# Values from weights three steps old, and in front of the scores, in a fused top-k attention and SMeLU MLP kernel

## The chip, the cores and the metric

The kernel runs on one core of one Trainium2 chip. The metric is device time in microseconds (us), lower is better: the median of the timed runs is 1606.17 us (three runs, 1605.85 to 1606.31).

A core has engines with queues of their own: TensorE (PE, with its weight loads shown apart as PEld), VectorE (DVE), ScalarE (ACT), GpSimd (POOL) and SyncE (SP), which here issues all DMAs. Each engine works through its instructions in program order and waits at an instruction until its semaphores are there.

## The reference

Eight batches of eight heads, 576 tokens of 64 numbers each; everything is float32. In each row of the scores only the 32 largest count. The attention's output, heads side by side, is the input of an MLP of 4608 x 512 x 2048 x 512 with a smoothed ReLU between.

```python
scores = scale * np.matmul(q, k.transpose(0, 1, 3, 2))           # (8, 8, 576, 576)
kth = np.partition(scores, -32, axis=-1)[..., -32:-31]
scores = np.where(scores >= kth, scores, -1000000000.0)
attn = np.exp(scores - np.max(scores, axis=-1, keepdims=True))
attn = attn / (np.sum(attn, axis=-1, keepdims=True) + 1e-09)
x = np.matmul(attn, v).transpose(0, 2, 1, 3).reshape(4608, 512)
h = x @ w_in                                                     # 512 -> 2048
g = np.where(h >= 1, h, np.where(h <= -1, 0.0, (h + 1) ** 2 / 4))
return g @ w_out                                                 # 2048 -> 512
```

## The kernel before

The attention is cut into 144 *steps*. A step takes 128 rows of queries of two heads (the 576 rows of a head are four tiles of 128 and a tail of 64; the tails of four heads share a step). For each step there are, in this order:

- *scores* (`scores`, L272): eight matmuls `sp`, two PSUM tiles, copied and scaled to `s` by ACT (L287);
- the *top 32* on DVE (`weights` and `first_top`, L310 and L345): the first part of step m+1 (`more` and `less`, L300, the first maxima, and ACT's `nmax` and `Exp` into `e`, L321 and L323) is woven into the last part of step m. It ends with L386, which zeroes what lies below the 32nd value and sums the rest;
- *division* by the sum on POOL (`divide`, L339), in the first place of the next step;
- *transposition* of the weights: in most steps by DMA (`move_w`, L412). ACT splits `e` into 16-bit halves (`halves`, L416, two copies), SP writes them to DRAM as `rows` (L418), and a transposing DMA brings them back as `wT` (L419). In the early steps and the last two it is done by TensorE (`transpose_w`, L395, with a diagonal matrix `diag` that ACT makes, L336);
- *values* (`values`, L425): 20 matmuls, or 40 short ones for tails, into a PSUM tile `po`, which ACT copies to `xT` (L446, L448).

When all heads of 128 rows are through, the rows are a *chunk* (36 in all), and `mlp` (L457) puts its MLP work into a queue `pending`: 8 hidden groups (`ph`, eight matmuls; then `r` and `g` by ACT and POOL, L470 to L484) and 16 output products (`py`, one matmul each, L489; then ACT copies `y`, L492, and SP stores it, L494). The last eight output products of the chunk before are woven in behind the first four hidden groups, two behind each; so when only those are left, a new chunk's first hidden group comes next on PE.

The order of PE, DVE, ACT and POOL is written out by the loop at L661; the order of SP is made by the framework's scheduler. A step has seven *places* (`slot` 0 to 6, so the third place is slot 2). Each place takes a part of the top-k work, then what is due there, and ends with `advance`, which takes MLP work from `pending` by a planned share. In the late steps (after all weights are converted, `early` false) the places of the loop before are:

- place 2: transposes of the next queries (`pq`) and, every second step, of the next batch's keys (`pk`, `pkt`); ACT copies them to `qT` and `kT`;
- place 3: `move_w` of step m-1;
- place 4: in odd steps the inspection of a piece of the weights' high words (`inspect_piece`, two `Sign` instructions with a sum, L168); in even steps the load of the next piece (`raw`, L126);
- place 5: the scores of step m+2, then the values of step m-2.

PSUM tiles: `sp`, `pq`, `pk`, `pw` share two buffers (tag "a"); `ph` and `po` share three; `py` has one. `s` and `e` have three buffers, `wT` has two in the late steps.

Of the kernel before, what the change touches and what calls it, by code (L numbers as in the profile page):

```python
# [10 lines left out]
F32 = mybir.dt.float32  # L11
# [3 lines left out]
AF = mybir.ActivationFunctionType  # L15
# [9 lines left out]
def kernel(  # L25
# [10 lines left out]
    nc = tc.nc  # L36
# [3 lines left out]
    P = 128  # L40
# [79 lines left out]
    def load(pool, i, bufs=3):  # L120
        if i < n_pieces and i not in loaded:
            if room and i < 28:
                loaded[i] = room[i % 8]
            else:
                loaded[i] = pool.tile([P, 2 * WC], U32, name="raw", bufs=bufs)
            nc.sync.dma_start(out=loaded[i], in_=pieces_of_weights[i][1].bitcast(U32))  # L126

    def words_of(pool, i, bufs=3):
        load(pool, i, bufs)
        words = loaded.pop(i).rearrange("p (n t) -> p n t", t=2)  # L130
        return words[:, :, 0], words[:, :, 1]
# [30 lines left out]

    def inspect_piece(pool, i):

        _, hi = words_of(pool, i, 2)
        for x in range(2):
            sign = pool.tile([P, WC], F32, name="sign", bufs=1)
            nc.scalar.activation(sign, hi.bitcast(F32), AF.Sign, bias=tiny[:, x:x + 1],  # L168
                                 accum_out=signs[:, x, i:i + 1])


    def run(ctx, paired):
# [157 lines left out]
        def divide(st):  # L330
            rz = att.tile([P, 2], F32, name="rz")
            nc.vector.reciprocal(rz, st["z"])
            if st["by_tensor"]:
                st["rz"] = diag = (late or words).tile([P, 2, P], F32, name="diag", bufs=1)
                for i in range(2):
                    nc.scalar.activation(diag[:, i, :], ident, AF.Copy, scale=rz[:, i:i + 1])  # L336
            else:
                for i in range(2):
                    nc.gpsimd.tensor_scalar(st["e"][:, i, :], st["e"][:, i, :], rz[:, i:i + 1], 1.0, ALU.mult, ALU.mult)  # L339
            if paired:  # L340
                m, seconds, kth = st["m"], st["seconds"], st["kth"]
                nc.gpsimd.tensor_tensor(out=excess[:, 2 * m:2 * m + 2], in0=seconds[:, 8:9 + SPLIT:SPLIT], in1=kth[:, LAST:7:-SPLIT],
                                        op=ALU.subtract)
# [50 lines left out]

        def transpose_w(st):  # L395
            w = st["e"]
            st["wT"] = wT = (late or words).tile([P, BLOCKS, P], F32, name="wT", bufs=2 if late else 1)
            pt = ps.tile([P, 2, NT, P], F32, name="pw", tag="a", bufs=2)
            for i in range(2):
                for c in range(NT):  # L400
                    nc.tensor.matmul(pt[:, i, c, :], w[:, i, main(i)][:, c * P:(c + 1) * P], st["rz"][:, i, :],  # L401
                                     start=True, stop=True)
            for i in range(2):
                nc.scalar.copy(wT[:, i * (NT + 1):i * (NT + 1) + NT], pt[:, i])
            pt = ps.tile([P, P], F32, name="pwt", tag="a", bufs=2)
            for i in range(2):
                nc.tensor.matmul(pt[i * TL:(i + 1) * TL, :], w[:, i, tail(i)], st["rz"][:, i, :], start=True, stop=True)
            nc.scalar.copy(wT[:, NT], pt)
# [1 line left out]


        def move_w(st):  # L412
            st["wT"] = wT = late.tile([P, BLOCKS, P], F32, name="wT", bufs=2)
            halves = late.tile([P, 2, 2 * S], U16, name="halves")
            for i in range(2):
                nc.scalar.copy(halves[:, :, i * S:(i + 1) * S], st["e"][:, i, :].bitcast(U16).rearrange("p (k t) -> p t k", t=2))  # L416
            rows = dram.tile([P, 2, 2 * S], U16, name="rows")
            nc.sync.dma_start(out=rows, in_=halves)  # L418
            nc.sync.dma_start_transpose(wT.bitcast(U16), rows.rearrange("p t k -> (p t) k"))  # L419
# [37 lines left out]
        def mlp(xT, rows, pool, last):  # L457
            gs, group = {}, 1 if last else GROUP
            py = []

            def hidden(x):
                ph = ps.tile([P, group, P], F32, name="ph", tag="ph", bufs=3)
                for i in range(group):
                    f = x * group + i
                    for kk in range(NK):
                        nc.tensor.matmul(ph[:, i], w_in[:, kk, f * P:(f + 1) * P], xT[:, kk],  # L466
                                         start=(kk == 0), stop=(kk == NK - 1))

                r = pool.tile([P, GROUP, P], F32, name="r", bufs=2)[:, 0:group]
                nc.scalar.activation(r, ph, AF.Relu, bias=half, scale=0.5)  # L470
                gs[x] = g = pool.tile([P, GROUP, P], F32, name="g", bufs=2 * LAG)[:, 0:group]
                if last:
                    nc.vector.tensor_scalar(g, ph, -1.0, 0.0, ALU.add, ALU.max)
                    nc.scalar.activation(r, r, AF.Square)
                    nc.vector.scalar_tensor_tensor(out=g, in0=r, scalar=1.0, in1=g, op0=ALU.min, op1=ALU.add)
                    return
                nc.scalar.activation(g, ph, AF.Relu, bias=minus, scale=1.0)  # L477
                if converted < n_pieces and x % 2:
                    nc.scalar.activation(r, r, AF.Square)
                    nc.gpsimd.tensor_scalar(r, r, 1.0, 0.0, ALU.min, ALU.max)  # L480
                else:
                    nc.gpsimd.tensor_scalar(r, r, 1.0, 0.0, ALU.min, ALU.max)  # L482
                    nc.gpsimd.tensor_tensor(out=r, in0=r, in1=r, op=ALU.mult)  # L483
                nc.gpsimd.tensor_tensor(out=g, in0=r, in1=g, op=ALU.add)  # L484

            def final(f):
                if f == 0:
                    py.append(ps.tile([P, DM], F32, name="py", tag="py", bufs=1))
                nc.tensor.matmul(py[0], gs[f // group][:, f % group], w_out[:, f, :], start=(f == 0), stop=(f == NF - 1))  # L489
                if f == NF - 1:  # L490
                    y = (late or words).tile([P, DM], F32, name="y", bufs=2)
                    nc.scalar.copy(y, py[0])  # L492
                    for p0, p1, dst in rows:
                        nc.sync.dma_start(out=dst, in_=y[p0:p1])  # L494

            behind = []
            while pending and pending[-1][3]:
                behind.insert(0, pending.pop())  # L500
            for x in range(NF // group + LAG):
                if x < NF // group:
                    pending.append((NK * group, needed(x * group + group - 1, False), partial(hidden, x), False))
                if x < LAG:
                    for _ in range(min(GROUP, len(behind))):
                        pending.append(behind.pop(0)[0:3] + (False,))
                else:
                    for f in range((x - LAG) * group, (x - LAG + 1) * group):
                        pending.append((DM // P, needed(f, True), partial(final, f), x >= NF // group))
# [151 lines left out]
        for m in range(n + 2):  # L661
# [6 lines left out]

            share, left = (total - spent) / (n + 2 - m), sum(x[0] for x in pending)
            for r in sorted(ready):  # L670
                if r + 3 > m and r >= valued:
                    share = min(share, left / (r + 3 - m))
                    left += NK * NF + NF * DM // P
            top_k, parts = None, [0] * SLOTS
            if m < n:
# [7 lines left out]
            for slot in range(SLOTS):  # L683
# [3 lines left out]
                if m < n and converted < n_pieces:  # L687
                    if slot in now_converting:
                        convert(now)
                elif slot == 3 and late is not None:  # L690
                    if m % 2:
                        inspect()
                    elif paired:
                        load(late, inspected, 2)
                if slot == 1 and 1 <= m <= n and state[m - 1]["by_tensor"]:
                    pe_time = max(pe_time, done[m - 1] + 2.0) + 1.0
                    transpose_w(state[m - 1])
                    ready_at[m - 1] = pe_time + 1.8
                if slot == 2 and 1 <= m <= n and not state[m - 1]["by_tensor"]:
                    move_w(state[m - 1])  # L700
                    ready_at[m - 1] = done[m - 1] + 14.0
                if slot == 2 and m == n and paired:
                    judge(ps, att)
                if slot == 2 and (early or m == first_late or m >= n - 1):
                    values_until(m)
                if m == 0 and slot in (1, 2):
                    next(first)
                if slot == 4:
                    begin_at(m + 2)
                    if not early:  # L710
                        values_until(m - 1)
                if slot == (6 if early else 1):
                    queries(m + 3)
                    if m < n and prep is None and next_keys < B and steps[m][0] == next_keys - 1 and steps[m][1] >= 1:
# [61 lines left out]
```

## Time and profile before

| | us |
|---|---|
| median of the timed runs | 1606.17 |
| the profiled execution | 1610.32 |
| its span, first to last instruction | 1608.5 |
| PE busy | 1514.0 |
| DVE busy | 1422.1 |
| ACT busy | 1140.4 |
| POOL busy | 943.3 |

The mean granted TensorE clock is 0.977 of full speed: 0.78 in the first 100 us, 0.90 in the second, 1.00 from there to 1400 us and 0.98 after.

How to read it: the page gives busy time, share of the span and instructions per engine, then the span in 40 slices (a digit is a busy share in tenths). A row of a group has the line, engine and operation, output<-input by the program's names, shapes and count, then busy time, mean ns of one, and the idle time of the engine in front of them with what ended it. A matmul in float32 leaves two records, so 8 instructions of `ph` are 16 records. Matmuls overlap, and a mean of one is longer than the distance of two. A row of a timeline has start, length, and in brackets the idle time before it.

### The profile page before, as it was taken

What the parts mean: (1) busy time and instruction counts of PE and PEld (TensorE: products, weight loads), DVE (VectorE), ACT (ScalarE), POOL (GpSimd) and SP (SyncE); (2) the same over time, 40 slices, a digit from 0 to 9 for tenths busy, and PEclk for the clock granted to TensorE, in tenths of its full rate; (3) what the DMA queues carried; (4) which work ended last, traced back from release to release, by engine and by line L of the source; (5) the groups of instructions that cost most, each with busy time, mean ns of one, the idle gap of its engine ahead of it and who ended that gap; (6) DMA issues with size and microseconds to landing.
All of it is one profiled execution on the core that took longest, in us unless ns stands there. A gap on an engine that the chain in (4) does not pass through costs nothing.

```text
span 1608.5 us, 32395 instructions
## 1 busy us (share of the span) xinstructions
PE 1514.0 (94%) x10925; PEld 1080.7 (67%) x10925; DVE 1422.1 (88%) x4443; ACT 1140.4 (71%) x2308; POOL 943.3 (59%) x1376
## 2 busy tenths in 40 slices
PE   5587999999999999999999999999999999999988
PEld 4465676777667776777667767766666667666665
DVE  7999889999998998999999998999898998889932
ACT  5677567777777767777768877776677776677632
POOL 5766466666555665655556666555555665556640
PEclk7798999999999999999999999999999999999999
DMA  9433246565465556665565545655565555544410
GB/s 252 132 96 110 72 130 174 157 158 153 133 174 161 154 143 173 161 150 145 145 172 159 160 133 157 172 143 140 135 174 146 142 142 130 145 131 126 123 51 16
DMA packets 439056, 227.92 MB, mean 142 GB/s; under 512 B 393056, under 2 KB 401248, under 8 KB 438880
## 3 DMA queue, kind: packets, MB, share of 16 engines
q1 hardware_dynamic: 438880, 225.75, 51.8%
q8 instruction: 88, 1.44, 0.4%
q14 instruction: 88, 0.72, 0.1%
HBM read 62.91 MB, written 86.11 MB: 93 GB/s over the span
## 4 chain that ended last, share of the span: by engine, by line
PE 71%; ACT 13%; POOL 4%; DVE 4%; DMA 4%; issue 3%; SPq 1%; POOLq 0%; ACTq 0%; DVEq 0%
PE ph L466 27%; PE py L489 24%; PE sp L285 8%; PE po L433 7%; ACT halves L416 3%; ACT e L323 3%; DMA wT<-rows 2%; ACT s L287 2%; ACT sign L168 2%; PE pw L401 1%; POOL e L339 1%; POOL r L483 1%; PE po L441 1%; ACT r L470 1%; POOL g L484 1%
## 5 line engine op out<-in xcount | busy, mean ns | idle before, releaser
L466 PEld LDWEIGHTS ph<-xT,w_in 128*128 128x128 f32 x4608 | 554.4, 192 | 118.3 <-issue 79.8
L466 PE MATMUL ph<-xT,w_in 128*128 128x128 f32 x4608 | 576.1, 278 | 14.8 <-ACT xT L446 12.9
L489 PE MATMUL py<-w_out,g 128*128 128x512 f32 x1152 | 558.6, 601 | 7.3 <-ACT y L492 7.1
L482 POOL TENSOR_SCALAR r<-r 128x256 f32<-128x256 f32 x276 | 150.7, 546 | 526.5 <-ACT r L470 526.1
L307 DVE MATCH_REPLACE8 more<-tops,more 128x288 f32<-128x288 f32 x864 | 375.2, 437 | 0.0
L416 ACT COPY halves<-e 128x1152 uint16<-128x1152 uint16 x260 | 288.0, 1153 | 112.7 <-POOL e L339 111.5
L470 ACT ACTIVATE r<-ph,half 128x256 f32<-128x256 f32 (+1 forms) x296 | 139.0, 470 | 241.1 <-PE ph L466 227.9
L489 PEld LDWEIGHTS py<-w_out,g 128*128 128x128 f32 x1152 | 193.5, 191 | 137.0 <-issue 131.2
L386 DVE SCALAR_TENSOR_TENSOR e<-s,kth,e 128x577 f32<-128x577 f32 x288 | 249.2, 900 | 0.1
L484 POOL TENSOR_TENSOR g<-r,g 128x256 f32<-128x256 f32 x280 | 219.6, 784 | 22.0
L323 ACT ACTIVATE e<-s,nmax 128x576 f32<-128x576 f32 x288 | 217.4, 770 | 4.7
L339 POOL TENSOR_SCALAR e<-e,rz 128x576 f32<-128x576 f32 x260 | 218.6, 851 | 0.0
L483 POOL TENSOR_TENSOR r<-r 128x256 f32<-128x256 f32 x276 | 201.5, 730 | 23.0
L300 DVE TENSOR_TENSOR more<-s 128x576 f32<-128x576 f32 x144 | 114.9, 798 | 109.0 <-ACT s L287 108.6
L287 ACT ACTIVATE s<-sp 128x576 f32<-128x576 f32 x288 | 169.2, 638 | 4.5 <-PE sp L285 4.2
L285 PE MATMUL sp<-kT,qT 64*128 64x288 f32 x1024 | 162.0, 433 | 9.9 <-ACT kT L244 9.0
L285 PEld LDWEIGHTS sp<-kT,qT 64*128 64x128 f32 x1024 | 89.6, 188 | 98.9 <-issue 29.1
L433 PE MATMUL po<-wT,v_in 128*64 128x128 f32 x2048 | 145.9, 282 | 10.3 <-DMA wT<-rows 7.9
L433 PEld LDWEIGHTS po<-wT,v_in 128*64 128x64 f32 x2048 | 113.4, 139 | 60.5 <-issue 37.5
L477 ACT ACTIVATE g<-ph,minus 128x256 f32<-128x256 f32 x280 | 131.8, 471 | 0.0
L348 DVE MAX8 tops<-more 128x8 f32<-128x288 f32 x288 | 125.4, 442 | 0.0
L300 DVE TENSOR_TENSOR less<-s 128x576 f32<-128x576 f32 x144 | 117.4, 815 | 0.0
(92 smaller groups left out, 1528.2 us busy)
## 6 DMA issues: line engine op xcount, KB each, us to landing
rows<-halves SPq DMA_DIRECT2D x130, 576.0 KB, 2.8
raw<-in_moe_w_out_dram SPq DMA_DIRECT2D x52, 256.0 KB, 2.8
raw<-in_moe_w_in_dram SPq DMA_DIRECT2D x48, 256.0 KB, 2.9
k_in<-in_k_dram SPq DMA_DIRECT2D x64, 128.0 KB, 3.2
q_in<-in_q_dram SPq DMA_DIRECT2D x32, 256.0 KB, 3.3
v_in<-in_v_dram SPq DMA_DIRECT2D x8, 1024.0 KB, 5.9
out_dram<-y SPq DMA_DIRECT2D x32, 256.0 KB, 3.0
kT<-in_moe_w_in_dram SPq DMA_DIRECT2D x16, 256.0 KB, 4.6
```

Of the source, the lines that this page charges most:

```text
L285: nc.tensor.matmul(o[:, a0 - c0:a1 - c0], qT[d, g, :], kT[d, g, k0:k0 + a1 - a0], start=True, stop=True)
L300: nc.vector.tensor_tensor(out=x, in0=s[:, :, 0:SH], in1=s[:, :, SH:S], op=op)
L307: nc.vector.match_replace(out=st["rest"][:, i, :], in_to_replace=eight(st["tops"], i, r - 8), in_values=src[:, i, :], imm_value=LOWEST)
L323: nc.scalar.activation(e[:, i, :], s[:, i, :], AF.Exp, bias=nmax[:, i:i + 1])
L339: nc.gpsimd.tensor_scalar(st["e"][:, i, :], st["e"][:, i, :], rz[:, i:i + 1], 1.0, ALU.mult, ALU.mult)
L386: nc.vector.scalar_tensor_tensor(out=st["all"][1][:, i, :], in0=st["all"][0][:, i, :], scalar=last[i], in1=st["all"][1][:, i, :], op0=ALU. ...
L416: nc.scalar.copy(halves[:, :, i * S:(i + 1) * S], st["e"][:, i, :].bitcast(U16).rearrange("p (k t) -> p t k", t=2))
L433: nc.tensor.matmul(po[j * D:(j + 1) * D], v_in[:, h, c, :] if c < NT else v_tl[0][:, h, :], wT[:, block(j, c)], start=(c == 0), stop=(c == ...
L466: nc.tensor.matmul(ph[:, i], w_in[:, kk, f * P:(f + 1) * P], xT[:, kk], start=(kk == 0), stop=(kk == NK - 1))
L483: nc.gpsimd.tensor_tensor(out=r, in0=r, in1=r, op=ALU.mult)
L484: nc.gpsimd.tensor_tensor(out=g, in0=r, in1=g, op=ALU.add)
L489: nc.tensor.matmul(py[0], gs[f // group][:, f % group], w_out[:, f, :], start=(f == 0), stop=(f == NF - 1))
```

## The change

Six edits. (1) In the late steps the values come in the third place, in front of the scores, and are those of step m-3 (`values_until(m - 2)`). (2) The scores of step m+2 move from the fifth place to the third. (3) `move_w` moves from the third place to the fourth, behind the inspection. (4) The transposed weights `wT` get three buffers. (5) The pacing of the MLP work counts a chunk's values one step later. (6) To make room: the signs are written over the low words of the inspected piece, `raw` has one buffer, `y` has one, and `diag` shares one with `halves`. Line numbers from L168 on are one smaller in the changed kernel.

```diff
     def inspect_piece(pool, i):
-        _, hi = words_of(pool, i, 2)
+        lo, hi = words_of(pool, i, 1)
         for x in range(2):
-            sign = pool.tile([P, WC], F32, name="sign", bufs=1)
-            nc.scalar.activation(sign, hi.bitcast(F32), AF.Sign, bias=tiny[:, x:x + 1],
+            nc.scalar.activation(lo.bitcast(F32), hi.bitcast(F32), AF.Sign, bias=tiny[:, x:x + 1],
                                  accum_out=signs[:, x, i:i + 1])
...
-                st["rz"] = diag = (late or words).tile([P, 2, P], F32, name="diag", bufs=1)
+                st["rz"] = diag = (late or words).tile([P, 2, P], F32, name="diag", tag="halves", bufs=1)
...
-            st["wT"] = wT = (late or words).tile([P, BLOCKS, P], F32, name="wT", bufs=2 if late else 1)
+            st["wT"] = wT = (late or words).tile([P, BLOCKS, P], F32, name="wT", bufs=3 if late else 1)
...
-            st["wT"] = wT = late.tile([P, BLOCKS, P], F32, name="wT", bufs=2)
+            st["wT"] = wT = late.tile([P, BLOCKS, P], F32, name="wT", bufs=3)
...
-                    y = (late or words).tile([P, DM], F32, name="y", bufs=2)
+                    y = (late or words).tile([P, DM], F32, name="y", bufs=1)
...
-                if r + 3 > m and r >= valued:
-                    share = min(share, left / (r + 3 - m))
+                if r + 4 > m and r >= valued:
+                    share = min(share, left / (r + 4 - m))
...
-                        load(late, inspected, 2)
+                        load(late, inspected, 1)
...
-                if slot == 2 and 1 <= m <= n and not state[m - 1]["by_tensor"]:
+                if slot == 3 and 1 <= m <= n and state[m - 1] is not None and not state[m - 1]["by_tensor"]:
                     move_w(state[m - 1])
-                    ready_at[m - 1] = done[m - 1] + 14.0
+                    ready_at[m - 1] = done[m - 1] + 15.0
...
-                if slot == 4:
+                if slot == 2 and not early:
+                    values_until(m - 2)
+                if slot == (4 if early else 2):
                     begin_at(m + 2)
-                    if not early:
-                        values_until(m - 1)
```

## The prediction

> **What bounds the kernel now.** I read the profile page first: busy shares, slices, the chain of work that ended last. TensorE (PE) is busy for 94% of the span, and PE is 71% of that chain; its low slices are the first five.
>
> ```profile
> PE 1514.0 (94%) x10925; PEld 1080.7 (67%) x10925; DVE 1422.1 (88%) x4443; ACT 1140.4 (71%) x2308; POOL 943.3 (59%) x1376
> PE   5587999999999999999999999999999999999988
> DVE  7999889999998998999999998999898998889932
> PE 71%; ACT 13%; POOL 4%; DVE 4%; DMA 4%; issue 3%; SPq 1%; POOLq 0%; ACTq 0%; DVEq 0%
> ```
>
> Then the busy time by stretches. The diff moves work only in steps after the weights' conversion (the "late" steps, from about 180 us on), so 250 to 1500 us is where it acts.
>
> ```profile
> 250.00:500.00 250.00, 245.93 (x1795) 175.56 (x1794) 234.28 (x737) 187.38 (x371) 154.68 (x225) 1.00 0.60 159
> 500.00:750.00 250.00, 249.16 (x1871) 177.52 (x1871) 233.30 (x731) 188.33 (x370) 153.39 (x222) 1.00 0.58 154
> 750.00:1000.00 250.00, 245.94 (x1802) 173.67 (x1799) 231.13 (x733) 186.48 (x373) 157.06 (x222) 1.00 0.56 153
> 1000.00:1250.00 250.00, 237.85 (x1704) 168.22 (x1704) 227.04 (x706) 180.38 (x352) 143.97 (x214) 1.00 0.57 152
> 1250.00:1500.00 250.00, 242.58 (x1802) 170.94 (x1799) 226.29 (x710) 180.41 (x356) 146.32 (x212) 0.99 0.50 136
> ```
>
> The PE column sums to 1221.5 of 1250 us: 28.5 us of idle PE are all that a new order can win here. Two thirds stand after 1000 us. Who owns them is in the groups of that window (last figures: idle before, releaser):
>
> ```profile
> L466 PE MATMUL ph<-xT,w_in 128*128 128x128 f32 x3924 | 487.9, 277 | 14.6 <-ACT xT L446 12.7 <-ACT xT L448 1.9
> L489 PE MATMUL py<-w_out,g 128*128 128x512 f32 x982 | 476.2, 601 | 6.5 <-ACT y L492 6.4
> L285 PE MATMUL sp<-kT,qT 64*128 64x288 f32 x864 | 134.0, 429 | 0.0
> L433 PE MATMUL po<-wT,v_in 128*64 128x128 f32 x1680 | 114.9, 279 | 5.4 <-DMA wT<-rows 4.6 <-ACT halves L416 0.8
> ```
>
> With 2.1 us before line 441 (values of the tail rows, also for wT) this is 28.6: the first hidden product of a chunk waits for xT, the first output product for the copy y of the previous chunk, the values for the transposed weights. Scores wait for nothing. DVE is not the bound: the waits give 108.6 us in which it wants scores, 97.6 of them in this window.
>
> ```profile
> DVE more L300 <- ACT s L287: 108.6, 89, 4.9
> ```
>
> Why xT is late shows in the timeline around the second-longest such wait. ACT:
>
> ```profile
> 1186.73 0.21 ACT L321 ACTIVATE nmax<-tops 128x2 f32<-128x2 f32 x1
> 1186.98 0.78 ACT L323 ACTIVATE e<-s,nmax 128x576 f32<-128x576 f32 x1
> 1187.66 0.52 ACT L168 ACTIVATE sign<-raw,tiny 128x256 f32<-128x256 f32 x1
> ...
> 1188.82 0.76 ACT L323 ACTIVATE e<-s,nmax 128x576 f32<-128x576 f32 x1
> 1189.49 1.16 ACT L287 ACTIVATE s<-sp 128x576 f32<-128x576 f32 x2
> 1190.55 0.26 ACT L446 COPY xT<-po 128x128 f32<-128x128 f32 x1
> ```
>
> and PE:
>
> ```profile
> 1187.56 0.39 PE L433 MATMUL po<-wT,v_tail 128*64 128x128 f32 x4
> 1187.87 0.94 PE L466 MATMUL ph<-xT,w_in 128*128 128x128 f32 x6
> 1190.86 1.38 PE L466 MATMUL ph<-xT,w_in 128*128 128x128 f32 x10 [2.05 <-ACT xT L446]
> ```
>
> The values end at 1187.95, but ACT, in program order, first does halves, maximum, both exponentials, two signs and the scores' copy: xT comes 2.6 us late (median over the window's xT copies, start after the values' end: about 2.0 us). PE has nothing else queued in front of the hidden product.
>
> **The change part by part.** A step is 1250/121 = 10.3 us (121 "more" instructions in the window), a place 10.3/7 = 1.5 us. No instruction is added or removed; the moved ones take their durations with them, so PE's sum stays 1514 us. PE pays about 93 ns at each switch between scores, values and full products (output-to-scores starts 523 ns apart against 429 without a switch, hidden-to-scores 205 against 112). Runs of one kind number 440 before and 439 after in the built order: zero.
>
> 1. *Values ahead of scores.* Both are in place 3 now, and the built order puts scores between the values and a chunk's hidden product in all late chunks but one. Scores last 1.24 us (8 matmuls). Were xT exactly as late as now, ten waits of 1.57, 1.29, 1.31, 2.05, 1.22, 1.26, 0.76, 1.86, 2.16 and 1.04 us would leave what exceeds 1.24: 0.33+0.05+0.07+0.81+0.02+0.62+0.92 = 2.8. On ACT xT now stands in front of the scores' copy (1.16), nmax, the exponentials, signs and halves, so it should be earlier; the best is 0. Gain between 11.8 and 14.6; I take 13.2.
>
> 2. *Weights three steps old, halves one place later.* The transposing DMA starts one place later, its reader comes five later (place 5 of step k+2 to place 3 of step k+3): 4 x 1.5 = 5.9 us more slack, against a longest wait of 3.52 us. SP's queue is in order: halves' write (landing 2.8 us) and the transposition (median 4.7, at most 8.8) stand behind loads of k, q, v that wait for PE; a third wT buffer keeps the next transposition from waiting for the reader that is now a step later. With two it would wait a step. Gain 7.5 (5.4+2.1); bounds 4.5 (the loads hold SP as much longer as the slack grew for the 3.5 us case) and 7.5. I take 7.5.
>
> 3. *Halves on ACT.* Now 111.5 us of ACT wait for POOL's division in front of halves (103.0 in the window). A place later, behind xT, the scores' copy and an exponential, POOL has had some 2 to 3 us more. Behind that wait stand g and r for POOL, and the copies that free PSUM. It costs PE nothing directly; ACT is 28% idle.
>
> 4. *Output product.* Its wait for y (one PSUM bank py) occurs where only one hidden group (1.95 us) separates two chunks: 17 boundaries before, 18 after in the built orders; five waits, 6.5 us. ACT has less queued ahead of y if point 3 holds: 5.5 left, gain 1.0; bounds 5 lost to 5 won.
>
> 5. *Scores right behind the transposes of q and k.* These stay in place 2 and share the two PSUM buffers "a" with the scores, now one place on instead of three. Cover before: typically a hidden group and two output products, 3.8 us, and the scores' wait is 0.0. Cover after: the values (1.3) and mostly one output product (0.5 to 0.9). ACT must do kT (2 x 0.58) or qT (0.59) in it. Best 0. Worst, ACT lagging by today's median 2.0 us: 2.0+1.16-2.2 = 0.95 for the 24 steps of the window with k and 2.0+0.59-2.2 = 0.4 for the 33 with q: 36 us. I take 2, close to the 0.0 row: the five microseconds of ACT work that make today's lag come after this place, with two hidden groups' time to drain.
>
> 6. *Scores two places earlier for DVE.* s of step m+2 overwrites that of m-1, whose last reader (line 386) is at the end of step m-1: three places clear. DVE has 97.6 us of wait to give in this window, so it can follow a PE that is 20 us quicker.
>
> 7. *Single buffers.* y: rewritten some 42 us later, its store lands in 3.0 us. raw: loaded at even steps, read at odd ones, landing 2.9 of 10.3 us; the signs overwrite its low words instead of a tile (0.53 us each, 120 in the window; a strided output is not in the trace: 0 to 0.5 more each, on an ACT with 28% idle). diag shares with halves in the last two steps: 0 to 2.8 us. All taken at 0; were raw's cover gone, ACT would stand 2.9 us every second step.
>
> 8. *Pacing.* MLP work is spread to a chunk's values a step later: three more output products and 24 more hidden ones stand behind the last transposes by PE (some 8 us), and at the hand-over two steps have no values. PE has queued MLP work in both places. 0, bounds -3 (all of today's 3.3 us of wT wait after 1500) to +5.
>
> Sum: -13.2 -7.5 -1.0 +2.0 = -19.7. The profiled execution is 1610.3 us (span 1608.5 and 1.8 around it): 1590.6. It stands 4.1 us above the median of the runs, 1606.17, so the forecast there is 1586.5.
>
> **Rules of the skill.** The row: the longest late gap, 3.52 us at 818.7, stands in a stretch with clock 1.00. The Trainium skill, "TensorE: Matmul & The Clock Gate", Part 1 (the HAM clock gate), has the array fall to half clock after an idle window of about 3.4 us, until it is busy as long again. By it that gap would cost about 1.7 us more (an estimate from that page) and the sum would be -21.4; the row shows no such drop. Against the reading of PE as the bound speaks the skill's "Perfetto Trace Analysis", Identifying the Most-Contended Engine: matmul busy time is no measure of the distance to the roofline, weight loads are. PEld is at 70% here. By it some 30% of the window would be free; but this change moves whole groups and leaves the spacing within them, so only gaps count.
>
> **Rivals.** (A) The forecast, 0.60; its own range 1579 to 1594. (B) Point 5 at about half a microsecond in the 24 k-steps (+12 in place of +2): 1596.5; chance 0.16. For it: the halved cover. Against: kT alone takes 1.16. (C) Slower: ACT's lag reaches place 2, because its cluster (nmax, exponentials, signs, halves: 5.3 us in odd steps) is now contiguous and k is transposed in the even step after it. At the worst price of 36 and gains of 21.7 that is +14, 1620. It decides from 21.7/57 = 0.38 us for each of these steps. Chance 0.14. Against: from the cluster to place 2 are over 4 us of mostly PE-paced ACT work. (D) No change, 1606: the waits for xT return one group later, as waits for a hidden group's PSUM (three buffers, shared with the values); 0.06. (E) All 28.5 us go: 1578; 0.04.
>
> This kernel's measurement tells about 0.2% (3.2 us) from no change. Faster: A, B, E, 0.80; within 0.2%: D, 0.06; slower: C, 0.14. The range reaches from 1576 (E, with a little at the end) to 1606 (B and D).
>
> **What would show it.** After: PE idle between 250 and 1500 us near 8; ph behind xT under 3 us; po behind wT 0; ACT xT starting under 1 us after the values; DVE's wait for s below 90; ACT's wait for POOL before halves below 60. Wrong if sp or its weight loads wait for kT or qT by tens of microseconds, or if DVE's busy share passes PE's.

## The result and the profile after

The changed kernel takes 1585.14 us (median of four runs, 1584.17 to 1585.86), the kernel before 1606.24 (four runs): a ratio of 0.9864, 95% interval 0.9847 to 0.9881. The forecast was 1586.5, in a range of 1576 to 1606. The profiled execution is 1584.77 us, its span 1583.0: 25.5 us shorter than the span before, of which some 4 us belong to the execution before, which lay above its median.

The page of the changed kernel, busy shares, TensorE's slices and the chain that ended last:

```profile
PE 1505.9 (95%) x10925; PEld 1076.7 (68%) x10925; DVE 1437.1 (91%) x4443; ACT 1153.5 (73%) x2308; POOL 938.2 (59%) x1376
PE   5586899999999999999999999999999999999998
PE 87%; ACT 6%; DVE 4%; issue 2%; DMA 1%; POOL 0%; SPq 0%; ACTq 0%; DVEq 0%; POOLq 0%
```

PE's share of the chain has gone from 71% to 87%; ACT's 13% are 6%, POOL's and the DMAs' 4% each are 0 and 1%. The stretches from 250 to 1500 us (columns: window, length, busy PE, PEld, DVE, ACT, POOL with counts, PE clock, DMA share, GB/s):

```profile
250.00:500.00 250.00, 250.00 (x1853) 180.01 (x1852) 245.94 (x749) 194.96 (x380) 155.18 (x230) 1.00 0.60 161
500.00:750.00 250.00, 246.04 (x1839) 173.93 (x1839) 233.20 (x729) 188.19 (x368) 154.43 (x219) 1.00 0.58 153
750.00:1000.00 250.00, 244.20 (x1761) 173.64 (x1759) 231.02 (x725) 188.19 (x364) 146.46 (x217) 1.00 0.58 152
1000.00:1250.00 250.00, 249.23 (x1831) 177.34 (x1831) 247.34 (x751) 195.41 (x380) 156.98 (x229) 1.00 0.63 164
1250.00:1500.00 250.00, 249.95 (x1865) 176.69 (x1864) 234.72 (x749) 188.56 (x365) 156.78 (x227) 1.00 0.53 140
```

The PE column leaves 10.6 us of idle PE (28.5 before), and what is left has moved: two thirds stood after 1000 us, now 9.8 of the 10.6 stand between 500 and 1000. The groups of the same window name the owner (last figures: idle before, releaser):

```profile
L465 PE MATMUL ph<-xT,w_in 128*128 128x128 f32 x3984 | 492.0, 277 | 0.0
L488 PE MATMUL py<-w_out,g 128*128 128x512 f32 x999 | 484.0, 600 | 9.7 <-ACT y L491 9.7
L284 PE MATMUL sp<-kT,qT 64*128 64x288 f32 x888 | 138.5, 429 | 0.1
L432 PE MATMUL po<-wT,v_in 128*64 128x128 f32 x1712 | 117.1, 279 | 0.8 <-DMA wT<-rows 0.8
```

The wait for xT is gone (14.6 to 0.0), and nearly all of that for the transposed weights (5.4, and 2.1 on the tails, to 0.8 and 0.0). Scores still wait for nothing. The output product's wait for y has grown from 6.5 to 9.7 and is now almost alone.

Why xT is in time, and why y is not, stands in one timeline. ACT:

```profile
668.36 1.17 ACT L243 COPY kT<-pk 64x512 f32<-64x512 f32 x2
670.37 0.27 ACT L445 COPY xT<-po 128x128 f32<-128x128 f32 x1 [0.83 <-PE po L432]
671.06 1.19 ACT L286 ACTIVATE s<-sp 128x576 f32<-128x576 f32 x2 [0.42 <-PE sp L284]
...
674.54 0.78 ACT L322 ACTIVATE e<-s,nmax 128x576 f32<-128x576 f32 x1
675.22 2.19 ACT L415 COPY halves<-e 128x1152 uint16<-128x1152 uint16 x2
677.32 0.77 ACT L322 ACTIVATE e<-s,nmax 128x576 f32<-128x576 f32 x1
678.00 0.56 ACT L491 COPY y<-py 128x512 f32<-128x512 f32 x1
```

and PE:

```profile
663.69 1.45 PE L488 MATMUL py<-w_out,g 128*128 128x512 f32 x3
...
673.31 1.88 PE L488 MATMUL py<-w_out,g 128*128 128x512 f32 x4
675.03 1.95 PE L465 MATMUL ph<-xT,w_in 128*128 128x128 f32 x16
678.70 1.10 PE L488 MATMUL py<-w_out,g 128*128 128x512 f32 x2 [1.72 <-ACT y L491]
```

ACT stands idle for 0.83 us until PE's values end, and at 670.37 copies xT at once. Over the window the copy starts 0.05 us (median) after the values' end; before it was 2.12, and for a tenth of the copies more than 3.49. The y copy has the old fate of xT: the chunk's last product ends at about 675.2, but ACT does both halves and an exponential first, and starts y at 678.00. One hidden group (1.95 us) lies on PE between the two chunks; the rest of the delay is a wait of 1.72.

Two more things moved, ACT's wait at halves (first row before, second after) and a wait of DVE (after), whole span:

```profile
L416 ACT COPY halves<-e 128x1152 uint16<-128x1152 uint16 x260 | 288.0, 1153 | 112.7 <-POOL e L339 111.5
L415 ACT COPY halves<-e 128x1152 uint16<-128x1152 uint16 x260 | 285.0, 1142 | 1.3 <-POOL e L338 1.3
L299 DVE TENSOR_TENSOR more<-s 128x576 f32<-128x576 f32 x144 | 114.0, 792 | 37.4 <-ACT s L286 37.0
```

ACT waited 111.5 us for POOL's division in front of halves, now 1.3. DVE waited 108.6 us for scores, now 37.0; it gave up 72 us of waiting and took 26.3 new ones, at line 385, for ACT's exponential.

The account of the 25.5 us. Idle PE in the three stretches (0 to 250, 250 to 1500, the rest) was 52.1, 28.5 and 5.6 and is 56.2, 10.6 and 2.1: 17.3 less. The other 8.1 are PE's busy time, which the prediction held to be constant: 1514.0 and 1505.9 us for the same 10925 matmuls. Two stretches of half clock late in the trace before, told of at the end, make up to 3.4 of them; for the remaining 4.7 no cause is shown. A matmul's end in the trace is modelled and overlaps the next start, so the idle time in front of a waiting matmul is somewhat shorter than what the wait cost: counted from start to start, against the usual distance of the same pair of matmuls, the waits between 250 and 1500 us cost 32.0 us before and 13.5 after.

### The profile page after: what moved, and what is told of

The parts are those of the page before. It is cut to its first block, busy times and chain, and to the rows that moved or that the text cites. A ratio compares the mean times of both kernels' runs of the same rounds, so it can differ in the third digit from the quotient of the medians.

```text
span 1583.0 us, 32547 instructions
## 1 busy us (share of the span) xinstructions
PE 1505.9 (95%) x10925; PEld 1076.7 (68%) x10925; DVE 1437.1 (91%) x4443; ACT 1153.5 (73%) x2308; POOL 938.2 (59%) x1376
## 4 chain that ended last, share of the span: by engine, by line
PE 87%; ACT 6%; DVE 4%; issue 2%; DMA 1%; POOL 0%; SPq 0%; ACTq 0%; DVEq 0%; POOLq 0%
PE ph L465 32%; PE py L488 30%; PE sp L284 11%; PE po L432 9%; ACT halves L415 2%; PE pw L400 1%; PE po L440 1%; PE pq L263 1%; DMA wT<-rows 1%; PE pk L239 1%; DVE bits L147 1%; ACT e L322 1%; ACT s L286 1%; DVE more L306 1%; ACT units L140 0%
## 5 line engine op out<-in xcount | busy, mean ns | idle before, releaser
L481 POOL TENSOR_SCALAR r<-r 128x256 f32<-128x256 f32 x276 | 140.3, 508 | 505.4 <-ACT r L469 505.3
L385 DVE SCALAR_TENSOR_TENSOR e<-s,kth,e 128x577 f32<-128x577 f32 x288 | 268.2, 960 | 26.5 <-ACT e L322 26.3
L483 POOL TENSOR_TENSOR g<-r,g 128x256 f32<-128x256 f32 x280 | 227.3, 812 | 22.0
L338 POOL TENSOR_SCALAR e<-e,rz 128x576 f32<-128x576 f32 x260 | 231.7, 901 | 0.0
L322 ACT ACTIVATE e<-s,nmax 128x576 f32<-128x576 f32 x288 | 222.5, 773 | 4.7
L286 ACT ACTIVATE s<-sp 128x576 f32<-128x576 f32 x288 | 173.7, 648 | 69.4 <-PE sp L284 62.7
L482 POOL TENSOR_TENSOR r<-r 128x256 f32<-128x256 f32 x276 | 190.5, 690 | 23.0
L432 PEld LDWEIGHTS po<-wT,v_in 128*64 128x64 f32 x2048 | 111.0, 136 | 70.1 <-issue 28.5
L347 DVE MAX8 tops<-more 128x8 f32<-128x288 f32 x288 | 125.6, 444 | 0.0
L319 DVE MAX8 tops<-more 128x8 f32<-128x288 f32 x288 | 116.6, 444 | 0.0
```

The source lines that it names most:

```text
L286: nc.scalar.activation(s[:, :, c0:c1], sp[:, :, 0:SH], AF.Copy, scale=SCALE)
L322: nc.scalar.activation(e[:, i, :], s[:, i, :], AF.Exp, bias=nmax[:, i:i + 1])
L385: nc.vector.scalar_tensor_tensor(out=st["all"][1][:, i, :], in0=st["all"][0][:, i, :], scalar=last[i], in1=st["all"][1][:, i, :], op0=ALU. ...
L432: nc.tensor.matmul(po[j * D:(j + 1) * D], v_in[:, h, c, :] if c < NT else v_tl[0][:, h, :], wT[:, block(j, c)], start=(c == 0), stop=(c == ...
```

## The experiments

Three groups were run, each on one chip beside the kernel before: the first four (before: 1608.47 us), the next four (1609.6), the last three (1609.45). They are compared by their ratio to it. The theory at the start was the prediction's: scores between values and hidden product hide xT, and older values give the transposition slack. The rival: xT is early because of its place on ACT, and what ACT has in front of it (halves, POOL's division) decides.

**The order of scores and values alone undone.** From the changed kernel; both stay in the third place.

```diff
-                if slot == 2 and not early:
-                    values_until(m - 2)
                 if slot == (4 if early else 2):
                     begin_at(m + 2)
+                    if not early:
+                        values_until(m - 2)
```

> The changed kernel with the two calls of place 3 exchanged: scores first, values behind them, so a chunk's hidden product again stands directly behind the values. Theory (the order: 1.24 us of scores cover the way over xT): the waits of ph for xT return, to the 14.6 us they had in the late steps, and the time rises by 11 to 14 us, to about 1598. Rival (the place: ACT has nothing queued in place 3, xT now starts 0.05 us after the values end in the median, against 2.0 before): ph waits only for the rest of the scores' copy and xT itself, 0.3 to 0.5 us at some 10 chunks, 3 to 5 us in all, about 1589.

Measured: 1587.75 us, 0.987 (0.985 to 0.9889), as the whole change within the intervals. Groups of 250 to 1500 us:

```profile
L465 PE MATMUL ph<-xT,w_in 128*128 128x128 f32 x3968 | 490.0, 277 | 0.0
L284 PE MATMUL sp<-kT,qT 64*128 64x288 f32 x888 | 142.0, 432 | 4.3 <-ACT kT L243 4.0
```

The hidden product has no scores in front of it and still waits for nothing: in the third place xT's lag is 0.05 us without any cover. What the values in front do is cover kT: without them the scores wait 4.3 us. The theory that scores between values and hidden product hide xT fell for this kernel; the place does it.

**The place alone undone.** From the changed kernel, values and scores go back to the fifth place, in the new order.

```diff
-                if slot == 2 and not early:
-                    values_until(m - 2)
-                if slot == (4 if early else 2):
+                if slot == 4:
+                    if not early:
+                        values_until(m - 2)
                     begin_at(m + 2)
```

> The changed kernel with values and scores, in the new order, moved back together from the third to the fifth place; values still three steps old, three buffers. Theory (the order covers): xT lags by about 2 us again behind halves and exponentials on ACT, but only what exceeds the scores' 1.24 us shows, about 3 us in the late steps: about 1588, and the wait for y stays near 10. Rival (the place): xT lag and the wait of ph for xT are back, 10 us and more: 1595 or above.

Measured: 1571.16 us, 0.977 (0.9751 to 0.9789), 1% below the whole change; neither side had foreseen that. The groups:

```profile
L465 PE MATMUL ph<-xT,w_in 128*128 128x128 f32 x3984 | 493.4, 277 | 1.6 <-ACT xT L445 1.6
L488 PE MATMUL py<-w_out,g 128*128 128x512 f32 x1005 | 481.7, 598 | 1.1 <-ACT y L491 1.1
```

xT's lag is back at 2.41 us (median), but now the scores cover it: 1.6 us of wait. And the wait for y is gone. So order and place are two remedies for the same wait, each nearly enough while halves come late, and the place seems to have a price of its own: in the third place, as the timeline of the changed kernel shows, a chunk can end where ACT is about to enter the cluster of exponentials and halves, and y stands behind it.

**Halves back in the third place.** From the changed kernel.

```diff
-                if slot == 3 and 1 <= m <= n and state[m - 1] is not None and not state[m - 1]["by_tensor"]:
+                if slot == 2 and 1 <= m <= n and state[m - 1] is not None and not state[m - 1]["by_tensor"]:
                     move_w(state[m - 1])
-                    ready_at[m - 1] = done[m - 1] + 15.0
+                    ready_at[m - 1] = done[m - 1] + 14.0
```

> The changed kernel with halves back in the third place, ahead of values and scores on ACT. Theory: ACT waits for POOL's division in front of halves by 100 us in all again (1.3 in the changed kernel), xT lags by 2 us or more, scores reach DVE later; of the lag the scores cover 1.24 us, PE waits before ph 3 to 6 us: 1588 to 1591. Rival: ACT's 27% of idle time absorbs all of it, 1585.

Measured: 1615.04 us, 1.0037 (1.0018 to 1.0057): slower than the kernel before, 1.7% above the changed one, and far above what both sides had expected. The hidden product waits for xT again, and y's wait is about as in the changed kernel (9.7):

```profile
L465 PE MATMUL ph<-xT,w_in 128*128 128x128 f32 x3875 | 484.3, 278 | 17.5 <-ACT xT L445 14.5 <-ACT xT L447 2.9
L488 PE MATMUL py<-w_out,g 128*128 128x512 f32 x975 | 479.4, 608 | 9.3 <-ACT y L491 9.3
```

ACT and PE around one of the waits for xT:

```profile
1234.65 0.74 ACT L252 COPY kT<-pkt 64x256 f32<-64x256 f32 x2
1237.46 2.20 ACT L415 COPY halves<-e 128x1152 uint16<-128x1152 uint16 x2 [2.06 <-POOL e L338]
1239.69 0.27 ACT L445 COPY xT<-po 128x128 f32<-128x128 f32 x1
```

```profile
1233.97 0.39 PE L432 MATMUL po<-wT,v_tail 128*64 128x128 f32 x4
1234.68 1.53 PE L284 MATMUL sp<-kT,qT 64*128 64x288 f32 x8 [0.32 <-ACT kT L243]
1236.13 0.94 PE L465 MATMUL ph<-xT,w_in 128*128 128x128 f32 x6
1240.01 2.29 PE L465 MATMUL ph<-xT,w_in 128*128 128x128 f32 x9 [2.94 <-ACT xT L445]
```

The values end at 1234.4. ACT, in program order, waits 2.06 us for POOL at halves, does 2.20 us of them, and only then copies xT, 5.3 us late. Scores and the group's first three matmuls, which read earlier parts of xT, cover 2.4 us of it. In this place a part of ACT's wait at halves (142 us in the window, 138 of them for POOL) is paid by PE. Idle PE in the window is 16.8 us more than in the changed kernel, and the waits bring 27.3 us of half clock there, where the changed kernel has none (see the end); that costs up to 13.7 us more.

**Three output products behind a hidden group.** The changed kernel's remaining wait is at y; this puts the eight held-back products as three, three and two behind the first three hidden groups instead of two behind each of four, so that two hidden groups lie between a chunk's last product and the next one's first.

```diff
-                    for _ in range(min(GROUP, len(behind))):
+                    for _ in range(min(GROUP + 1, len(behind))):
```

> The changed kernel with the last eight output products of a chunk woven in three, three and two behind the next chunk's first three hidden groups in place of two behind each of four, so that two hidden groups (3.9 us) stand between the last output product of a chunk and the first of the next, in place of one (1.95). Theory (the wait for y is a single PSUM bank that one hidden group is too short to clear): PE's wait of py for y, 12.3 us in the profile of the changed kernel, falls to 0 to 2, and the time by 9 to 12 us, to 1573 to 1576. Rival: PE does not get it back, since DVE at 98% in some stretches or PSUM of the hidden groups takes it: 1582 to 1586.

Measured: 1568.46 us, 0.9752 (0.9734 to 0.9771), the fastest kernel of this study and below the expected 1573 to 1576. The group:

```profile
L488 PE MATMUL py<-w_out,g 128*128 128x512 f32 x1006 | 482.9, 600 | 0.0
```

The wait is gone, and the span is 16.8 us shorter than the changed kernel's, more than the 9.7 us of idle: PE idles 53.8, 1.0 and 0.8 us in the three stretches, so 2.4 were gained before 250 us and 1.3 at the end; counted from start to start, the window's waits cost 13.5 us and now cost 2.2, 11.3 less. One stretch of half clock fewer before 250 us (61.4 us of it in place of 64.9) makes up to 1.7.

**The order alone**, put into the kernel before.

```diff
                 if slot == 4:
-                    begin_at(m + 2)
                     if not early:
                         values_until(m - 1)
+                    begin_at(m + 2)
```

> The kernel before with one exchange: in the fifth place the values of step m-2 come ahead of the scores of step m+2. Places, age of the weights and buffers are as before. Theory (either of two things is enough to hide xT: scores as cover, or a place where ACT has nothing queued): xT keeps its lag of about 2 us, but the wait of ph for xT falls from 14.6 to about 3 us; the values read wT 1.3 us earlier, so the wait for wT grows from 7.5 to 9 to 13; in all 6 to 10 us less, about 1598. Rival (the order does nothing, the gain is all the place's): 1606, with xT's wait still above 10.

Measured: 1609.04 us, 1.0006 (0.999 to 1.0023). The groups:

```profile
L466 PE MATMUL ph<-xT,w_in 128*128 128x128 f32 x3935 | 488.5, 277 | 3.9 <-ACT xT L446 2.7 <-ACT xT L448 1.1
L433 PE MATMUL po<-wT,v_in 128*64 128x128 f32 x1682 | 115.2, 279 | 12.7 <-DMA wT<-rows 12.0 <-ACT g L477 0.2
```

The prediction's first step is seen in pure form: 14.6 us of xT waits become 3.9 (its worst case said 2.8), with the lag at 2.45 us. But most of it is given back: the values now come before the scores, and wait for the transposed weights, 12.7 us in place of 5.4 (2.9 in place of 2.1 on the tails). The window's idle PE falls by 2.9 us only, that before 250 us is 4.0 more, and in all nothing is won. The waits moved as the theory said; the time is the rival's.

**The age alone.** The changed kernel with halves in the third place (as above), and in the fifth place first the scores, then the values of step m-3.

```diff
-                if slot == 2 and not early:
-                    values_until(m - 2)
-                if slot == (4 if early else 2):
+                if slot == 4:
                     begin_at(m + 2)
+                    if not early:
+                        values_until(m - 2)
```

> The changed kernel with order and places of the kernel before: halves in the third place, scores and then values in the fifth; kept are values from weights three steps old, three wT buffers, the pacing and the single buffers. Theory: the wait of po for wT goes (7.5 us) but the wait of ph for xT stays or grows, since 17 chunk starts instead of 14 now stand directly behind the values: 1600 to 1608. Rival (the age is what makes the change fast): 1590 or below.

Measured: 1604.47 us, 0.9964 (0.9953 to 0.9974). The mirror image:

```profile
L465 PE MATMUL ph<-xT,w_in 128*128 128x128 f32 x3920 | 489.7, 278 | 21.0 <-ACT xT L445 18.2 <-ACT xT L447 2.7
L432 PE MATMUL po<-wT,v_in 128*64 128x128 f32 x1680 | 114.9, 279 | 0.0
```

The values wait 0.0 for weights, and the hidden product 21.0 us for xT in place of 14.6. What is left, 0.36%, is 5.8 us.

**Two buffers for wT** in the changed kernel.

```diff
-            st["wT"] = wT = (late or words).tile([P, BLOCKS, P], F32, name="wT", bufs=3 if late else 1)
+            st["wT"] = wT = (late or words).tile([P, BLOCKS, P], F32, name="wT", bufs=2 if late else 1)
...
-            st["wT"] = wT = late.tile([P, BLOCKS, P], F32, name="wT", bufs=3)
+            st["wT"] = wT = late.tile([P, BLOCKS, P], F32, name="wT", bufs=2)
```

> The changed kernel with two buffers of wT in place of three. The prediction said that the next transposition would then wait a step for its reader. Theory now: the buffer is read in place 3 and the next halves are made in place 4 of the same step, so the transposition waits for PE at most about a place, and is still two steps ahead of its own reader: PE's wait for wT stays under 1 us, 1583 to 1588. Rival (the waiting transposition holds up SP's queue, and loads and halves with it): above 1592, with po waiting for wT.

Measured: 1584.6 us, 0.9845 (0.9829 to 0.9861), no slower than with three; the wait for weights in the window is 0.9 us. The third buffer buys nothing here.

**Fifth place and three products together**, the edits of the second and the fourth experiment.

> Both variants that came out faster than the changed kernel together: values and scores in the fifth place (values first, three steps old), and the last eight output products woven three, three and two. Theory: both removed the same thing, the wait of py for y (9.7 us to 1.1 and to 0.0), so together they give what the second alone gives, 1566 to 1570. Rival (place five has a gain of its own, 4 us or more): 1564 or below.

Measured: 1570.6 us, 0.9758 (0.9741 to 0.9774): no better than either alone (0.977 and 0.9752), as expected if both remove the same wait; y's is 0.0 here.

**Order and age, places as before.** The fifth-place kernel with halves in the third place.

> The changed kernel with values and scores in the fifth place and halves in the third, both as in the kernel before; kept are the order (values first), the age of three steps, the pacing and the single buffers. Only the place of halves differs from the run with values and scores in the fifth place. Theory (order and age are a pair: the order alone took 11 us of waits for xT away and gave 5 us of waits for wT, the age alone did the reverse): no wait for wT, about 3 us for xT, ACT waits some 100 us for POOL again behind nothing that PE needs: 1572 to 1580. Rival (halves' later place carries the gain, as it seemed to where halves stood directly ahead of xT): 1590 or above.

Measured: 1586.38 us, 0.9854 (0.9829 to 0.9879), between what the two sides said, and just what the whole change gives. The values wait 0.0 for weights, the hidden product 6.2 us for xT and the output product 3.6 for y:

```profile
L465 PE MATMUL ph<-xT,w_in 128*128 128x128 f32 x3971 | 493.7, 278 | 6.2 <-ACT xT L445 6.1
L488 PE MATMUL py<-w_out,g 128*128 128x512 f32 x998 | 479.8, 599 | 3.6 <-ACT y L491 3.5
L415 ACT COPY halves<-e 128x1152 uint16<-128x1152 uint16 x246 | 271.7, 1152 | 118.3 <-POOL e L338 117.1 <-DMA rows<-halves 0.3
```

The last row is what sets it apart from the fifth-place kernel, where ACT waits 9.5 us at halves, PE 1.6 for xT and 1.1 for y.

**Halves later alone**, put into the kernel before (the third experiment's edit, reversed).

> The kernel before with one change: halves in the fourth place, behind the maximum, one exponential and the signs, in place of the third. Theory: ACT's wait for POOL before halves (111.5 us) nearly goes, but xT stays in the fifth place behind all of that work, so its wait stays above 10 us, and wT comes later by up to a place for a reader that is not moved: 5 to 10 us more of wT waits: 1600 to 1612. Rival (ACT's wait for POOL was what made xT late): xT waits below 5 us and 1595 or less.

Measured: 1635.02 us, 1.0164 (1.0137 to 1.0192), slower than expected. The values, two steps old, wait for the transposition that starts a place later:

```profile
L433 PE MATMUL po<-wT,v_in 128*64 128x128 f32 x1648 | 114.4, 281 | 29.7 <-DMA wT<-rows 28.7 <-ACT sign L168 0.8
```

**Three products alone**, put into the kernel before (the fourth experiment's edit).

> The kernel before with the last eight output products of a chunk woven three, three and two. Theory: the wait of py for y (7.3 us) goes and the other waits stay: 1598 to 1602. Rival (the time goes into the waits for xT or wT, which are nearest): 1604 to 1608.

Measured: 1615.89 us, 1.0043 (1.0019 to 1.0067), above what both sides expected. The wait for y is gone (6.5 to 0.0), and that for xT is 23.3 us in place of 14.6, that for the weights 7.7 in place of 5.4: more was lost at these than was won. The longer waits also bring 20.5 us of half clock into the window in place of 3.4, worth up to 8.5 us. Why the waits grow beyond what y gave back is open; ACT's wait at halves rose with them, 104 to 127 us.

The runs that move values, scores and halves, as per cent of the kernel before. The rows with values three steps old have the changed pacing and buffers too, which no run has by themselves:

| values | scores | halves | time |
|---|---|---|---|
| 2 steps old, place 5, after scores | place 5 | place 3 | 0 (the kernel before) |
| 2 old, place 5, **first** | 5 | 3 | +0.06 |
| **3 old**, place 5, after | 5 | 3 | -0.36 |
| **3 old**, place 5, **first** | 5 | 3 | -1.46 |
| 2 old, place 5, after | 5 | **4** | +1.64 |
| **3 old**, place 5, **first** | 5 | **4** | -2.30 |
| **3 old**, **place 3**, **first** | **3** | 3 | +0.37 |
| **3 old**, **place 3**, after | **3** | **4** | -1.30 |
| **3 old**, **place 3**, **first** | **3** | **4** | -1.36 (the change) |

## Why the prediction was right, and where its steps were not

The time is 1.4 us from the forecast, and rival A held. The sum was not as right as that, and part of the nearness is luck: in idle PE, xT gave 1.4 us more than its term, the weights 0.8 less, the scores 1.9 more and y 4.2 less, so the window gave 17.9 us where 19.7 stood; and PE's busy time, held to be constant, fell.

*Values ahead of scores* (13.2 gained; measured 14.6 of waits). The size was right, and the cover it argued with exists: the order alone left 3.9 of the 14.6. But in this change the cover decides nothing, as the kernel with scores first shows. What decides is what the text named second: in the third place ACT has nothing in front of xT. What the step left out is where the gain goes when it is alone: into the wait for weights, +0.06% in all.

*Weights three steps old* (7.5; measured 6.7 in the window, and 2.8 after 1500 us, where the text had put 0 with a bound of 3). Right, but the two steps were summed as if each could be had by itself. Alone they are +0.06% and -0.36%; together -1.46%. Most of each one's gain goes into the other's wait: the order alone took 10.7 us from xT's wait and gave 8.1 to the weights', the age alone took 7.5 from the weights' and gave 6.4 to xT's. That PE, ahead of its supplies, simply meets the next one is the likely reading; no run shows it by itself. The sum came out because the change makes both. "With two it would wait a step", of the buffers, has no price on PE: two do as well.

*Halves on ACT* ("it costs PE nothing directly"). This is the step that failed. ACT's wait for POOL went as foreseen (103.0 to 1.3 in the window), but it was put at 0 for PE, and the place of halves is worth 13 us in the fifth place (1.46% less against 2.30%) and some 28 in the third (0.37% more against 1.36% less), because there xT is queued on ACT behind it: its wait is 17.5 us against 0.0, while those for y (9.3 against 9.7) and kT (0.6 against 0.1) hardly differ. Half clock after these waits is a part of the 28. Taken without the older values the same edit costs 26 us. Cover by "28% idle" was the error: 111.5 us of ACT's 468 idle ones were this very wait, and idle time elsewhere does not help an xT that is queued behind it.

*Output product* (1.0 gained; measured 3.2 lost). The wrong sign, within the bounds of 5. The text supposed that less is queued ahead of y when POOL's wait is gone. But in the third place chunks end at the cluster, and the 2.19 us of halves themselves are in front. It is the largest term left: with that wait removed the kernel stands at 0.9752. The wait for y goes with the third place, wherever halves stand: 9.3 and 9.7 us there, 3.6 and 1.1 with values and scores in the fifth. That this is so because the chunks' ends move with the place is read from timelines; no run moved them alone.

*Scores behind the transposes* (2 lost; measured 0.1). Rivals B and C fell. The values do cover kT: with scores first 4.3 us appear, far from the 36 of the worst case.

*Scores earlier for DVE*, *single buffers*: DVE's wait fell from 97.6 to 31.3 in the window, and a sign into the low words lasts 0.53 us as before. *Pacing*: 4.1 us more idle before 250 us and 3.5 less after 1500 (2.8 of them the weights' wait); 0 was right in sum.

That 28.5 us were "all that a new order can win here" was too low. The fastest kernel is 2.48% (40 us) below the kernel before; idle PE over its whole span is 30.6 us less, a wait costs more than its idle column shows, and until PE's last matmul the half clock is 61.4 us in place of 71.7, worth up to 5.2 us. Rival E, all of it gone, was set at 1578; that kernel, not the change, passes it.

On the clock, the text took from one row (3.52 us of idle without a drop) that gaps here cost their length alone. Another row of the same trace speaks against it, which comes last. The other rule weighed there, the Trainium skill's "Perfetto Trace Analysis", Identifying the Most-Contended Engine, would judge the headroom by the weight loads (and by the share of peak FLOPs, which was not worked out here); the weight loads are at 881.6 of 1250 us (71%) in the changed kernel, and the matmuls' means, 277 and 600 ns, are as before (277 and 601). What moved with the time was PE's idle time, 28.5 to 10.6 us, and the half clock.

## What to carry to other kernels

On an engine that works in order, the lateness of a copy is set by what is queued directly in front of it, waits for other engines included; look there before trusting a busy share. Gains at two waits on one path are not to be summed before asking whether one removed only moves the time to the other: here the order alone was worth nothing and the age alone 0.36%, but both together 1.46%. After a move, look at what now falls at the old hot spot: here the next 17 us lay in one line, which sets how many hidden groups separate two chunks' output products.

## What the runs showed of the hardware

The granted clock falls to half after waits much shorter than the 3.4 us that the prediction weighed. In the kernel before, one wait of PE of 1.86 us (the hidden product for xT, until 1402.61) is followed by this (windows, columns as above):

```profile
1400.00:1404.00 4.00, 2.14 (x20) 1.91 (x17) 3.24 (x10) 2.53 (x7) 0.00 (x0) 1.00 0.66 208
1404.00:1408.00 4.00, 4.00 (x11) 1.94 (x11) 4.00 (x14) 1.35 (x3) 3.01 (x5) 0.57 0.42 95
```

and in its timeline by this:

```profile
1404.05 2.73 PE L489 MATMUL py<-w_out,g 128*128 128x512 f32 x3
```

Three output products take 2.73 us, where three at full clock take 1.45 (663.69 in the timeline above). The half clock lasts 3.41 us (6.83 in three cases of 28) and costs up to half of that. Over the 13 traces of this case, from 250 us to near the end, such a drop followed none of 206 waits from 0.1 to 1.75 us, 2 of 8 from 1.75 to 2.0, 10 of 16 from 2.0 to 2.25, 6 of 7 from 2.25 to 2.5, and 10 of 13 longer ones; the kernel before has two, the changed one none, the one with halves back in the third place eight. The Trainium skill, "TensorE: Matmul & The Clock Gate", Part 1, gives an idle window of about 3.4 us, free-running, as what drops the clock. The length of the drops agrees; that waits of 1.9 to 2.5 us suffice does not, and that the wait of 3.52 us passed without one shows that length alone doesn't decide.

What decides can be read from the clock's records in the traces. In each trace all changes of the clock lie on one grid of 3.41 us, which agrees with a free-running window. Of the grid's windows at full clock from 250 us on, half clock follows none of the 2218 in which PE idles up to 1.84 us, and 28 of the 29 with 1.86 us or more (the one without has 1.89). The wait of 3.52 us fell on two windows, with 1.68 (816.99 to 820.40) and 1.84 us of idle; that of 1.86 lay within one (1400.67 to 1404.08). So idle time within one window decides, and a little over half of the window is enough. In this kernel, then, a wait over 1.9 us may cost up to 1.7 us beside its own length, and removing long waits pays more than their sum.
